# Issuing the gate weights of K tile 2 from SyncE's queue instead of ScalarE's

## The chip, the cores and the metric

One core of a Trainium2 chip. The metric is device time in microseconds (us) of one execution; most executions of this kernel lie within 0.5 us of 179.3, so a change of a tenth of a microsecond is near what can be seen at all.

Engines are called as the profile calls them: PE is TensorE's matmul, PEld its weight load, DVE is VectorE, ACT is ScalarE, POOL is GpSimd, SP is SyncE. "SPq" and "ACTq" lines are DMA issues by those sequencers: their time is the time of issuing, not that of the data.

## The reference, cut to what matters

```
x  = A_x                                # [1, 2048, 512] bf16
xn = layernorm(x)
out = x + S5(xn) + (silu(xn @ w_gate) * (xn @ w_up)) @ w_down
# S5: a complex diagonal recurrence over the 2048 rows: Bu = xn @ B, scan, @ C, + xn * Dskip
```

The kernel works in four chunks of 512 rows, each of four tiles of 128 rows (x0 to x3 in the first chunk). The dimension of 512 that is summed over in xn @ w_gate is cut into four "K tiles" of 128.

## The kernel before

The kernel is a graph of tasks. PE's and SP's tasks stay in the order of the program; those of DVE, ACT and POOL are put in order by a list scheduler with a cost model, before the program is built. The loads at the start, each a DMA with a semaphore of its own:

```python
x_load(0)
x_load(1)                                                     # SyncE, 128 KB each
act_q = [dma("ld_touch", ..., eng="act")]                     # 64 bytes
act_q.append(wg_load("a0", 0, 2, eng="act", ...))             # K tiles 0 and 1 of w_gate, 448 KB
x_load(2)
act_q.append(wg_load("a1", 2, 3, eng="act", ...))             # K tile 2, 224 KB: the line that changes
wg_load("a2", 3, 4)                                           # K tile 3, SyncE
x_load(3)
pload("ld_ldt", ...); pload("ld_lim", ...); pload("ld_lre", ...)   # three parameter rows, 1 KB each
dma("ld_wu0", ...); dma("ld_wg1", ...); dma("ld_wu1", ...)    # w_up, rest of w_gate, rest of w_up
dma("ld_x4", x_sb[:, 4:8, :], ...)                            # x of the second chunk, 512 KB
# [...] cut
dma("ld_bre", BT[:, 0], A_B_re, ..., xpose=True)              # transposing DMAs; each of them
dma("ld_bim", BT[:, 1], A_B_im, ..., xpose=True)              # waits for all DMAs before it
act_table(AF.Sqrt, (act_q[-1],))                              # ACT's first table, behind its last load
```

The opening of VectorE. Statistics of x2 (first half) stand ahead of x1's reciprocal and normalisation; the order is fixed:

```python
("r", 0, 0), ("n", 0, 0), ("b", 1, 0), ("b", 1, 1), ("s", 1, 0), ("b", 2, 0),   # b: statistics
("r", 1, 0), ("n", 1, 0), ("n", 1, 1), ("b", 2, 1), ...                         # r: reciprocal, n: normalise
```

The opening of PE: dummy matmuls, then x0's transposes, then for the 128 rows of x0 seven matmuls on each K tile, with x1's transpose placed after the 18th, and so on. The first chunk's matmuls on the rest of w_gate and on w_up follow, then those that read the transposed B (called `BT`).

The scheduler's model of a DMA halves the bandwidth for a queue that is not SyncE's:

```python
dma_free[e] = xs + t.nbytes / (_DMA_BW if e == "sp" else 0.5 * _DMA_BW)
```

Of the kernel before, what the change touches and what calls it, by code (L numbers as in the profile page):

```python
# [249 lines left out]
def bass_parallel_sum__ssm_conv_s5__swiglu_ffn__prompt_kernel(  # L250
# [32 lines left out]
    with es:  # L283
# [109 lines left out]
        def dma(name, dst, src, writes, nbytes, reads=(), after=(), out_=False, eng="sp", xpose=False, prio=0.0, order=(), **kw):  # L393
            after = tuple(after)
            if xpose:
                after = after + tuple(dma_tasks)
                fn = lambda e, dst=dst, src=src: e.dma_start_transpose(out=dst, in_=src)
                est, nb = 1900.0, int(nbytes * 1.2) + 140000
            else:
                if xp_state[0] is not None:  # L400
                    after = after + (xp_state[0],)
                fn = lambda e, dst=dst, src=src: e.dma_start(dst, src, **kw)
                est, nb = 330.0 + nbytes / 900.0, nbytes
            t = g.add(eng, fn, reads=reads, writes=writes, name=name, dma=True, after=after, out=out_, est=est, nbytes=nb, prio=prio, order=order)
            dma_tasks.append(t)
            if xpose:
                xp_state[0] = t
            return t
# [9 lines left out]
        def x_load(a, **kw):  # L418
            return dma("ld_x%d" % a, x_sb[:, a:a + 1, :], x_v[:, a:a + 1, :], [("x", a)], TILEB, **kw)

        def wg_load(nm, k0, k1, **kw):
            return dma("ld_wg" + nm, wg[:, k0:k1, 0:FG], wg_v[:, k0:k1, 0:FG], [("wg", nm)], (k1 - k0) * 128 * FG * 2, **kw)
# [4 lines left out]
        act_q = [dma("ld_touch", tch[0:16, 0:1], wg_v[0:128:8, 0:1, 0:2], [("tch",)], 16 * 4, eng="act")]  # L427
        act_q.append(wg_load("a0", 0, 2, eng="act", order=(act_q[-1],)))
        x_load(2)
        act_q.append(wg_load("a1", 2, 3, eng="act", order=(act_q[-1],)))  # L430
        wg_load("a2", 3, 4)
        x_load(3)
        pload("ld_ldt", 2, A_log_dt)
# [657 lines left out]
```

## Time and profile before

| | before |
|---|---|
| median of 3 runs | 179.53 us (179.03 to 179.59) |
| span of the profiled run | 177.5 us |
| PE busy | 173.9 us, 98% |
| DVE busy | 162.5 us, 92% |

From the page of the kernel before: the span, the busy times, and the chain of work that ended last, by engine.

```profile
span 177.5 us, 2421 instructions
PE 173.9 (98%) x927; PEld 83.9 (47%) x935; DVE 162.5 (92%) x284; ACT 87.8 (49%) x116; POOL 9.3 (5%) x22
...
## 4 chain that ended last, share of the span: by engine, by line
PE 98%; issue 0%; DVE 0%
```

The chain is PE almost alone: what doesn't give PE an earlier start or take a hole out of it changes nothing.

The timeline of before (start, duration, engine, line, operation, destination and source, count; in brackets the idle time ahead of it and what ended it):

```profile
1.22 0.97 ACTq L402 DMA_DIRECT2D wg<-in_B_w_gate_dram  x2
2.17 0.43 SPq L402 DMA_DIRECT2D wg<-in_B_w_gate_dram  x1
2.22 1.28 ACT L466 ACT_TABLE_LOAD   x1 [2.22 <-issue]
...
5.04 0.44 SPq L402 DMA_DIRECT2D wu<-in_B_w_up_dram  x1
5.45 0.21 DVE L522 BATCH_NORM_AGGREGATE mv<-st 128x2 f32<-128x12 f32 x1
5.71 1.17 PE L803 MATMUL pb<-xnT,wg 128*128 128x128 bf16 x18
5.92 0.43 DVE L512 BATCH_NORM_STATS2 st<-x_sb 128x6 f32<-128x256 bf16 x1 [0.26 <-DMA x_sb<-in_A_x_dram]
6.44 0.60 DVE L517 TENSOR_SCALAR xn_sb<-x_sb,mv,rstd 128x256 bf16<-128x256 bf16 x2
6.84 0.29 PE L582 MATMUL pb<-ident,xn_sb 128*128 128x128 bf16 x2
...
12.93 1.03 PE L759 MATMUL pb<-xnT,wg 128*128 128x512 bf16 x4
15.47 2.47 DVE L482 BATCH_NORM_STATS2 st<-x_sb 128x6 f32<-128x512 bf16 x4 [2.39 <-DMA x_sb<-in_A_x_dram]
15.52 2.12 SPq L397 DMA_TRANSPOSE BT<-in_A_B_re_dram  x1
19.66 2.14 SPq L397 DMA_TRANSPOSE BT<-in_A_B_im_dram  x1
23.83 1.79 SPq L397 DMA_TRANSPOSE xnT<-xn_sb  x1
```

What to see: at 5.92 DVE had stood 0.26 us for x2. Behind that statistic wait x1's reciprocal and normalisation (6.44), and for these PE waits before x1's transpose at 6.84. Its 18 gate matmuls started 56 ns apart from 5.71 on, the last at 6.65, so 0.14 us of PE is lost there (start to start in the trace, less the usual spacing). Lower down is a second chain, which is off PE: when x4-7 has landed, at 15.44, B_re's transposing DMA goes out, and when that has landed B_im's at 19.66. That one lands at 23.81, and PE wants it at 25.02.

### The profile page before, as it was taken

Reading aid. Unit: us, or ns where it says so; the run is one execution under the profiler, and the core shown is the slowest. Engines: PE = TensorE matmul, PEld = TensorE weight load, DVE = VectorE, ACT = ScalarE, POOL = GpSimd, SP = SyncE. Lnnn points to the kernel's source line nnn. Section 1 sums busy time; section 2 is a strip of 40 time slices with the busy share of each in tenths; the row PEclk is TensorE's granted clock in tenths of the full one; section 3 lists DMA queues with packets and bytes.
Section 4 is the critical chain, followed back from the end, with each engine's and each line's share of the span. In section 5 each row is a group of like instructions: output and inputs, shape, how many; then the busy total and the mean of one; then the engine's idle time right before and its main releaser. Section 6 shows DMA issues by size and latency. Waiting matters only on the chain.

```text
span 177.5 us, 2421 instructions
## 1 busy us (share of the span) xinstructions
PE 173.9 (98%) x927; PEld 83.9 (47%) x935; DVE 162.5 (92%) x284; ACT 87.8 (49%) x116; POOL 9.3 (5%) x22
## 2 busy tenths in 40 slices
PE   8999999999999999999999999999999999999994
PEld 2894444444444444444444444444444444444743
DVE  2865999899999999999999999999899999999933
ACT  4679979789999665034565560000965520000000
POOL 3022300040000000310000000000000000000000
PEclk9999999999999999999999999999999999999999
DMA  5992694664951000002700000002000000001022
GB/s 155 326 365 67 139 124 96 167 132 101 358 123 24 0 0 0 0 30 69 126 18 0 0 0 4 0 30 76 12 0 4 0 0 0 0 0 53 10 89 89
DMA packets 22966, 12.37 MB, mean 70 GB/s; under 512 B 15180, under 2 KB 22956, under 8 KB 22956
## 3 DMA queue, kind: packets, MB, share of 16 engines
q1 hardware_dynamic: 22508, 11.54, 25.0%
q10 hardware_dynamic: 448, 0.69, 1.2%
q8 instruction: 7, 0.11, 0.3%
q14 instruction: 3, 0.02, 0.0%
HBM read 6.46 MB, written 2.10 MB: 48 GB/s over the span
## 4 chain that ended last, share of the span: by engine, by line
PE 98%; issue 0%; DVE 0%
PE pb L759 36%; PE pb L959 21%; PE pb L876 16%; PE pb L972 15%; PE pb L803 4%; PE pb L477 3%; PE pb L839 2%; PE pb L849 1%; PE pb L582 1%; DVE x_sb L977 0%
## 5 line engine op out<-in xcount | busy, mean ns | idle before, releaser
L916 DVE TENSOR_TENSOR_SCAN rot<-sm,car,rot 128x512 bf16<-128x512 f32 x32 | 39.0, 1266 | 0.1
L959 PE MATMUL pb<-wd,hT 128*128 128x512 bf16 (+3 forms) x194 | 38.1, 355 | 0.2
L759 PE MATMUL pb<-xnT,wu 128*128 128x512 bf16 x160 | 37.3, 380 | 0.0
L759 PE MATMUL pb<-xnT,wg 128*128 128x512 bf16 x132 | 31.3, 380 | 0.0
L972 PE MATMUL pb<-W,hss 128*128 128x512 bf16 (+2 forms) x140 | 28.1, 355 | 0.2
L876 PE MATMUL pb<-xnT,BT 128*128 128x512 bf16 x128 | 28.1, 379 | 0.0
L959 PEld LDWEIGHTS pb<-wd,hT 128*128 128x128 bf16 (+1 forms) x198 | 18.5, 98 | 19.9
L759 PEld LDWEIGHTS pb<-xnT,wu 128*128 128x128 bf16 x160 | 15.6, 98 | 18.9 <-issue 0.2
L771 ACT ACTIVATE sg<-pb 128x1024 bf16<-128x1024 f32 x20 | 20.1, 1024 | 8.6 <-PE pb L759 7.7
L829 ACT ACTIVATE uf<-pb 128x1024 bf16<-128x1024 f32 x20 | 20.5, 1026 | 7.2 <-PE pb L759 5.9
L972 PEld LDWEIGHTS pb<-W,hss 128*128 128x128 bf16 x144 | 13.5, 98 | 14.3
L759 PEld LDWEIGHTS pb<-xnT,wg 128*128 128x128 bf16 x132 | 12.7, 98 | 15.7 <-ACT xn_sb L506 0.4
L876 PEld LDWEIGHTS pb<-xnT,BT 128*128 128x128 bf16 x128 | 12.5, 98 | 15.1
L883 ACT ACTIVATE u_sb<-pb 128x1024 bf16<-128x1024 f32 x16 | 16.2, 1017 | 5.4 <-PE pb L876 5.4
L977 DVE TENSOR_TENSOR x_sb<-pb,x_sb 128x512 bf16<-128x512 f32 (+2 forms) x18 | 11.0, 623 | 3.5 <-PE pb L972 3.5
L831 DVE TENSOR_TENSOR hT<-sg,uf 128x1024 bf16<-128x1024 bf16 x20 | 13.3, 680 | 0.0
L506 ACT ACTIVATE xn_sb<-x_sb,nmr,rstd 128x512 bf16<-128x512 bf16 x8 | 6.0, 804 | 9.2 <-DVE nmr L503 9.2
L858 ACT ACTIVATE sg<-pb 96x1024 bf16<-96x1024 f32 x2 | 2.0, 1013 | 17.1 <-PE pb L839 17.1
L482 DVE BATCH_NORM_STATS2 st<-x_sb 128x6 f32<-128x512 bf16 x12 | 7.4, 681 | 3.1 <-DMA x_sb<-in_A_x_dram 3.1
L907 DVE TENSOR_TENSOR rot<-rot,cosT 128x2048 bf16<-128x2048 bf16 x8 | 9.7, 1215 | 0.1
L907 DVE TENSOR_TENSOR rot<-rot,sin 128x2048 bf16<-128x2048 bf16 x8 | 9.7, 1216 | 0.0
L907 DVE TENSOR_TENSOR rot<-u_sb,cosT 128x2048 bf16<-128x2048 bf16 x8 | 9.7, 1216 | 0.0
(81 smaller groups left out, 144.3 us busy)
## 6 DMA issues: line engine op xcount, KB each, us to landing
out_dram<-x_sb SPq DMA_DIRECT2D x15, 128.0 KB, 1.7
x_sb<-in_A_x_dram SPq DMA_DIRECT2D x3, 512.0 KB, 6.9
wd<-in_B_w_down_dram SPq DMA_DIRECT2D x1, 1280.0 KB, 6.3
wu<-in_B_w_up_dram SPq DMA_DIRECT2D x1, 768.0 KB, 5.5
wu<-in_B_w_up_dram SPq DMA_DIRECT2D x1, 608.0 KB, 7.6
x_sb<-in_A_x_dram SPq DMA_DIRECT2D x4, 128.0 KB, 3.5
wg<-in_B_w_gate_dram SPq DMA_DIRECT2D x1, 480.0 KB, 6.4
wg<-in_B_w_gate_dram ACTq DMA_DIRECT2D x1, 448.0 KB, 4.0
```

Of the source, the lines that this page charges most:

```text
L482: return g.add("dve", lambda e, a=a: e.bn_stats(out=st[:, a, :], in_=x_sb[:, a, :]), reads=[("x", a)], writes=[("st", a)], name="bnst%d" % ...
L759: inst = e.matmul(pbank[0:fs, bk, :].rearrange("p (j t) -> p j t", j=4), lhsT=w[:, kt, i * 128:i * 128 + fs], rhs=xnT[:, c % 2, :, kt, :], ...
L771: g.add("act", lambda e: e.activation(out=sg[rows, sl, 0:n, :].rearrange("p a t -> p (a t)"), in_=pair_f32(rows, bk, 512 * n), func=AF.Sil ...
L829: g.add("act", lambda e: e.activation(out=uf[rows, ul, 0:n, :].rearrange("p a t -> p (a t)"), in_=pair_f32(rows, bk, 512 * n), func=AF.Ide ...
L831: g.add("dve", lambda e: e.tensor_tensor(out=hT[rows, hb, i0:i0 + n, :], in0=sg[rows, sl, 0:n, :], in1=uf[rows, ul, 0:n, :], op=ALU.mult), ...
L876: inst = e.matmul(pbank[:, bk, :].rearrange("p (j t) -> p j t", j=4), lhsT=BT[:, ri, kt, pt * 128:(pt + 1) * 128], rhs=xnT[:, c % 2, :, kt ...
L883: g.add("act", lambda e: e.activation(out=u_sb[:, us].rearrange("p r t -> p (r t)"), in_=pair_f32(slice(0, 128), b0), func=AF.Identity), r ...
L907: tt = lambda out, a, b, op, r, w, nm: g.add("dve", lambda e: e.tensor_tensor(out=out, in0=a, in1=b, op=op), reads=r, writes=w, name="%s_% ...
L916: g.add("dve", lambda e, A0=A0, A1=A1, k=k, ri=ri, pt=pt: e.tensor_tensor_scan(out=A1[:, k, ri, :], data0=rr[:, pt:pt + 1].to_broadcast([1 ...
L959: inst = e.matmul(pbank[:, bk, 0:nc_], lhsT=hT[0:fs, hb, i, lt * 128:(lt + 1) * 128], rhs=wd[0:fs, i, c0:c0 + nc_], start=(i == 0), stop=F ...
L972: inst = e.matmul(pbank[:, bk, 0:nc_], lhsT=hss[:, hb, pt, ri, lt * 128:(lt + 1) * 128], rhs=W12[:, ri, pt, c0:c0 + nc_], start=False, sto ...
L977: g.add("dve", lambda e, bk=bk, a=a, c0=c0, nc_=nc_: e.tensor_tensor(out=x_sb[:, a, c0:c0 + nc_], in0=pbank[:, bk, 0:nc_], in1=x_sb[:, a, ...
```

## The change

Its intent: take K tile 2 off ScalarE's queue, where it follows 448 KB, and put it in SyncE's behind x2.

```diff
         x_load(2)
-        act_q.append(wg_load("a1", 2, 3, eng="act", order=(act_q[-1],)))
+        wg_load("a1", 2, 3)
         wg_load("a2", 3, 4)
```

## The prediction

> **What bounds the kernel now.** TensorE. The page gives PE 98% of the 177.5 us span, granted clock 1.00; the chain that ended last is PE 98%. After its opening PE issues almost without a hole, and DVE (92% busy) is ahead of it: the last half of hss is done at 165.3 us, wanted at 168.1; the last W at 70.1, wanted at 74.5. So only what moves PE's opening (before 13 us) or makes a new hole counts.
>
> **The opening, from timeline and DMA landings.** An issue costs a sequencer 0.41 to 0.50 us. K tile 2 (224 KB) is issued by ScalarE at 1.7 us and lands 4.5 us later, at 6.2; its first matmul starts at 6.5, the weight load about 0.1 earlier. K tile 3 lands at 6.8, wanted at 7.1. x2 lands at 5.9, x3 at 7.2. VectorE, done with x1's statistics, stands 0.26 us waiting for x2 (the waits name it), so x1's normalisation, queued behind x2's statistics, comes late, and PE has a hole of 0.14 us before x1's transpose at 6.87.
>
> **What the change does.**
> - SyncE's queue gains an issue, 0.45 us. Everything behind slips: first w_up half 10.55 to 11.0 (wanted 13.8), rest of w_gate 11.9 to 12.4 (wanted 12.9), x4-7 15.5 to 15.9, and the transposing DMAs that follow: B_im lands at 23.8, wanted about 25; x chunk 1's transpose at 29.2, wanted at 31.1. Each keeps 0.5 us or more: nothing charged to PE.
> - ScalarE loses 0.49 us of issue, so the Sqrt table load starts at 1.7, not 2.2. Its first use waits for x0's statistics, done at 3.85; table and warm-up are done at 3.81 already. Worth nothing.
> - K tile 2 is issued at 2.2, not 1.7. From 3.0 to 6.5 us the DMA engines are saturated (share 1.0, about 370 GB/s), so the backlog, not the issue, sets the landing. The Trainium skill, "DMA: Bandwidth & Descriptors", section "Issuing engines are not separate DMA queues", says that DMAs of all issuers run on the same 16 engines and interleave. The trace agrees: between 4.5 and 5.25 us packets of both queues move, x2's and ScalarE's. With K tile 2 behind x2, x2 shares less: estimate from the packets' rates, x2 lands 0.2 to 0.5 us earlier (5.4 to 5.7); K tile 2, now ahead of K tile 3 instead of beside it, at 5.9 to 6.3; K tile 3 and x3 unchanged.
>
> **On the critical path.** If x2 is earlier, the 0.14 us hole goes: about -0.14 us. If K tile 2 lands after 6.4, PE stalls by the difference, at worst about 0.3.
>
> **Side effect.** The kernel orders its instructions by a cost model that halves the bandwidth of ScalarE's queue. There K tile 2 gets earlier and everything behind it on SyncE 0.7 us later, so DVE's and ACT's orders after 12 us may change. With 2 us or more of DVE slack I expect little; a bad order could cost some tenths.
>
> **Prediction.** 179.4 us, 178.9 to 180.2 eight times in ten. Faster by over 2%: 0.01; within 2%: 0.97; slower: 0.02.
>
> **What would show it.** DVE's wait for x2 gone or shorter; PE's hole before 6.87 gone; K tile 2 landing before 6.4; w_up landing about 0.45 us later; the DVE wait for x4-7 0.4 us longer; PE contiguous afterwards.
>
> **What would make it wrong.** SyncE's queue alone filling K tile 2 slower than two queues together (a PE hole at 6.4); w_gate's rest after 12.9; a new order that delays evacuations of PSUM, with PE waiting for ACT or DVE.

## The result

| | before | after |
|---|---|---|
| median of 6 runs | 179.48 us (179.03 to 179.59) | 179.17 us (179.01 to 179.59) |
| ratio to before (95% interval) | | 0.9993 (0.9977 to 1.001) |

A ratio here is the mean time of one kernel's runs over that of the other's of the same rounds, so it isn't quite the ratio of the medians. Executions over 1.5% slower than the fastest of the same kernel are left out of the means. The change is inside the noise. When both were run again later (below, `after_again` and `before_again`), after came out at 1.0008 and before, against itself, at 1.0007.

The profile after, page and timeline:

```profile
span 177.7 us, 2429 instructions
PE 174.5 (98%) x935; PEld 84.3 (47%) x935; DVE 162.7 (92%) x284; ACT 87.6 (49%) x116; POOL 10.2 (6%) x22
```

```profile
1.23 0.45 ACTq L402 DMA_DIRECT2D wg<-in_B_w_gate_dram  x1
1.71 1.28 ACT L466 ACT_TABLE_LOAD   x1 [1.71 <-PEq L1076]
2.18 0.91 SPq L402 DMA_DIRECT2D wg<-in_B_w_gate_dram  x2
...
5.46 0.21 DVE L522 BATCH_NORM_AGGREGATE mv<-st 128x2 f32<-128x12 f32 x1
5.51 0.44 SPq L402 DMA_DIRECT2D wu<-in_B_w_up_dram  x1
5.58 0.37 DVE L512 BATCH_NORM_STATS2 st<-x_sb 128x6 f32<-128x256 bf16 x1
5.80 1.38 PE L803 MATMUL pb<-xnT,wg 128*128 128x128 bf16 x18
6.23 0.60 DVE L517 TENSOR_SCALAR xn_sb<-x_sb,mv,rstd 128x256 bf16<-128x256 bf16 x2
7.01 0.28 PE L582 MATMUL pb<-ident,xn_sb 128*128 128x128 bf16 x2
...
13.09 1.03 PE L759 MATMUL pb<-xnT,wg 128*128 128x512 bf16 x4
16.18 2.47 DVE L482 BATCH_NORM_STATS2 st<-x_sb 128x6 f32<-128x512 bf16 x4 [2.01 <-DMA x_sb<-in_A_x_dram]
16.24 2.15 SPq L397 DMA_TRANSPOSE BT<-in_A_B_re_dram  x1
20.54 1.84 SPq L397 DMA_TRANSPOSE BT<-in_A_B_im_dram  x1
24.52 2.82 SPq L397 DMA_TRANSPOSE xnT<-xn_sb  x1
```

Three things stand in these lines.

1. The predicted step came true on VectorE: it no longer waits for x2 (5.58, no bracket), and x1 is normalised 0.2 us earlier. PE has no hole before x1's transpose either, but that alone shows little: PE arrives there at 7.01, when even the old queue's x1 (PE was released at 6.84 in before) would have been ready.
2. Yet PE reaches that transpose 0.17 us *later* (7.01 against 6.84), because its 18 matmuls start 0.09 us later, behind slower dummies, and take 1.38 us and not 1.17. In the trace the first five of them start 107 ns apart and the others 56 ns: the clock of TensorE rose only at 6.2 us. In before it had risen at 5.3, ahead of the first of them. The Trainium skill, "TensorE: Matmul & The Clock Gate", section "Part 1: The HAM clock gate (the "warmup" mystery)", says that the clock doubles after some 3.4 us of activity, at the end of a window that runs free of the kernel, so that the moment differs from run to run. The traces agree: 107 and 56 ns at 128 columns, and a rise at 5.3, 4.3, 6.2 and 6.5 us in four profiles of the two kernels, with the same dummy matmuls in front. The mean granted clock shows nothing of it (1.00 for both kernels), because time without a clock record counts as 1.00: the trace of before has its first record at 5.30 us, that of before_again at 4.33, each at the rise, and those of after and after_again have none, so the profile page of after lacks the row. There only the spacing tells.
3. From the first 512-column matmul (12.93 and 13.09) to the end of the span (177.5 and 177.7) both kernels take 164.6 us, although the scheduler put DVE's work in another order (by line, operation and tile 21 of its 284 instructions stand elsewhere in the trace). The order cost nothing.

And the slip: w_up was issued at 5.51 instead of 5.04, x4-7 landed 0.7 us later, and B_im with it. That is more than the issue's 0.47. Half of x4-7's 512 packets had started by 12.93 and 13.02 us in two looks at before, and by 13.53 and 13.27 in two at after, so the bulk slipped about as the issue did; but it lands with its last few packets, which started at 14.77 and 14.72, and at 15.67 and 15.26. Why this tail was longer in after isn't shown.

### The profile page after: what moved, and what is told of

It reads as the page before. It is cut to its first block, busy times and chain, and to the rows that moved or that the text cites. A ratio compares the mean times of both kernels' runs of the same rounds, so it can differ in the third digit from the quotient of the medians.

```text
span 177.7 us, 2429 instructions
## 1 busy us (share of the span) xinstructions
PE 174.5 (98%) x935; PEld 84.3 (47%) x935; DVE 162.7 (92%) x284; ACT 87.6 (49%) x116; POOL 10.2 (6%) x22
## 4 chain that ended last, share of the span: by engine, by line
PE 98%; DVE 0%; issue 0%
PE pb L759 36%; PE pb L959 21%; PE pb L972 16%; PE pb L876 16%; PE pb L803 4%; PE pb L477 3%; PE pb L839 2%; PE pb L849 1%; PE pb L582 1%; DVE x_sb L977 0%
## 5 line engine op out<-in xcount | busy, mean ns | idle before, releaser
L959 PE MATMUL pb<-wd,hT 128*128 128x512 bf16 (+3 forms) x198 | 38.8, 355 | 0.0
L907 DVE TENSOR_TENSOR rot<-u_sb,cosT 128x2048 bf16<-128x2048 bf16 x8 | 9.7, 1216 | 0.0
L907 DVE TENSOR_TENSOR rot<-u_sb,sin 128x2048 bf16<-128x2048 bf16 x8 | 9.7, 1216 | 0.0
```

The lines of the kernel that those rows point to most:

```text
L907: tt = lambda out, a, b, op, r, w, nm: g.add("dve", lambda e: e.tensor_tensor(out=out, in0=a, in1=b, op=op), reads=r, writes=w, name="%s_% ...
L959: inst = e.matmul(pbank[:, bk, 0:nc_], lhsT=hT[0:fs, hb, i, lt * 128:(lt + 1) * 128], rhs=wd[0:fs, i, c0:c0 + nc_], start=(i == 0), stop=F ...
```

## The experiments

Two questions were open. Is the step from x2 worth anything to the time, and if so, what takes it back? The moment of the clock's rise disturbs both, so most runs are of a delayed pair in which it falls before any real matmul.

### d_before, d_after, d_move, d_order: the clock's rise taken out; queue and orders apart

```diff
         streams = _schedule(g.tasks, engs)
+        dly = g.add("dve", lambda e: e.memset(rot[:, 0], 0.0), name="delay")   # nobody uses it; first load at 4.15 us, not 0.79
+        streams["dve"].insert(0, dly)
+        # [...] the first load of each queue waits for dly; writers of rot too
+        streams["pe"].insert(1, ...)        # nine more dummy matmuls, so that PE stays busy
```

In d_move the orders are those of before, and afterwards K tile 2's issue alone is moved to SyncE behind x2. In d_order the orders are those of after, and its issue is put back on ScalarE behind the first two K tiles.

> The kernel before, with every load held back by a 3.2 us fill on VectorE and TensorE kept busy with 9 more dummy matmuls, orders unchanged. Theory A (the spread of the runs, 179.0 to 179.6, is the moment at which TensorE's clock rises, 5.3 us in the profile of before, about 6.2 in that of after): the rise now falls before the first real matmul (about 9 us) in every run, so the runs lie within 0.25 us of each other, about 3.3 us above before (182.3 to 183.0), and the hole of about 0.14 us in TensorE ahead of x1's transpose is there in the profile. Rival: the spread comes from the DMA or from elsewhere and stays 0.5 us.

> The changed kernel with the same delay. Theory A with the step x2 of the prediction: no wait of VectorE for x2, no hole ahead of x1's transpose, and 0.10 to 0.20 us faster than d_before. Rival 1 (x2's earlier landing buys nothing, the 0.3 us between the medians was luck of the clock): within 0.05 us of d_before. Rival 2 (issues behind K tile 2 slip by 0.45 us and cost TensorE something): slower than d_before, with a new hole after 13 us of the undelayed time.

> Delayed; the instruction orders of before on all engines, only K tile 2's issue moved from ScalarE's queue to SyncE's behind x2. If the DMA move is the cause: as d_after within 0.06 us (0.10 to 0.20 faster than d_before). If the new orders of VectorE and ScalarE are the cause: as d_before.

> Delayed; the instruction orders of after on all engines, K tile 2's issue put back on ScalarE's queue behind the first two K tiles. If the DMA move is the cause: as d_before within 0.06 us, with the hole ahead of x1's transpose. If the new orders are the cause: as d_after.

| run | orders | K tile 2 issued by | five runs, us | mean |
|---|---|---|---|---|
| d_before | before | ScalarE | 182.35 182.39 182.80 182.67 182.69 | 182.58 |
| d_order | after | ScalarE | 182.44 182.38 182.33 182.48 182.37 | 182.40 |
| d_after | after | SyncE | 182.34 183.22 182.58 182.81 182.73 | 182.74 |
| d_move | before | SyncE | 182.75 183.29 182.42 182.68 182.71 | 182.77 |

In all four traces the clock had risen by 5.9 us and the first gate matmul began at 9.0, as meant. But two expectations fell. The runs didn't draw together (0.45 us for d_before, 0.88 for d_after), so the clock isn't the whole of the spread. And SyncE's queue wasn't 0.10 to 0.20 us faster: its ten runs have a mean of 182.75, those of ScalarE's queue 182.49, though the two ranges overlap. The orders have no effect of one sign: with K tile 2 on ScalarE the new ones are 0.18 us better, on SyncE they are equal.

The profile of d_move shows what a longer run holds. Its timeline (the line numbers are a few higher, from the added lines):

```profile
19.89 1.94 SPq L397 DMA_TRANSPOSE BT<-in_A_B_re_dram  x1
24.25 1.93 SPq L397 DMA_TRANSPOSE BT<-in_A_B_im_dram  x1
27.25 1.03 PE L878 MATMUL pb<-xnT,BT 128*128 128x512 bf16 x4
28.48 1.41 PEld L878 LDWEIGHTS pb<-xnT,BT 128*128 128x128 bf16 x8 [0.69 <-DMA BT<-in_A_B_im_dram]
28.48 1.69 PE L878 MATMUL pb<-xnT,BT 128*128 128x512 bf16 x7 [0.20 <-DMA BT<-in_A_B_im_dram]
```

PE does the four matmuls on B_re and then stands for B_im: 0.36 us, start to start. That is nearly all of the 0.40 us by which this run (182.75) is longer than d_before's profiled one (182.35): from the first 512-column matmul to the end it takes 164.99 us, and the profiles of the other three 164.59 to 164.60. This is a hole far behind the opening, at the end of the chain x4-7, B_re, B_im on SyncE's queue, the queue to which the change adds an issue. The prediction had looked at this chain and charged nothing for it. Two smaller facts from the opening of these four: the hole before x1's transpose was 0.00 in d_before and 0.07 us in d_order, so it isn't there in every run of the old queue; and with SyncE's queue K tile 3 landed at 10.27 and 10.29 instead of 9.95 and 9.91, and opened a hole of about 0.05 us in PE. The next pair doesn't repeat that (10.26 with SyncE's queue, without a hole, and 10.29 with ScalarE's), so it isn't shown to come from the change.

One flaw of this family: B_re's issue came 0.39 us after x4-7 had landed, in all four, and only 0.08 us after it in before and after (SyncE's fifteen waits stood in another order). So the delayed kernels are closer to this hole than the real ones: without the extra 0.31 us d_move's hole would have been about 0.05 (an estimate from these two numbers).

### p_before and p_after: the wait for B taken out as well

```diff
+        # ten dummy matmuls (2.2 us) ahead of the first matmul that reads B
+        streams["pe"].insert(streams["pe"].index(b0), pad)
-                for d in t.deps:
+                for d in sorted(t.deps, key=lambda d: d.idx):     # waits in the order of the loads
```

> d_before with two more things, the same in both of this pair: ten dummy matmuls (about 2.2 us) ahead of the first matmul that reads B, so that no wait for the transposed B can show, and SyncE's waits put in the order of the loads. If the late B (hole of 0.36 us in d_move's profile) is what spread d_before's runs (182.35 to 182.80), they now lie within 0.2 us, about 184.5. If the spread comes from the opening, it stays 0.4 us.

> The changed kernel with the same delay, dummies and wait order. What is left between the two is the opening alone. The prediction's step (x2's earlier landing closes a hole of 0.14 us) would give 0.10 to 0.20 us faster. My theory now (the hole ahead of x1's transpose is there in some runs only, 0.14, 0.03 and 0.07 us in three profiles of the old queue, and K tile 3, now 0.3 us later, opens another of 0.05): equal within 0.08 us, and a spread under 0.2 us, while d_after spread over 0.88.

Measured: p_before 184.71, 184.77, 184.80, 184.88 (mean 184.79); p_after 184.72, 184.75, 184.78, 184.81, 184.91 (mean 184.79); both 1.0311 times before. The two are equal to 0.01 us, and the spread is 0.17 and 0.19 us. With the wait for B out of reach the difference between the queues is gone, and so is most of the spread. Two things were done at once here, the dummies and the order of the waits (on every engine); both keep PE from waiting for B, but they weren't tried apart. In p_after's profile B_im's transposing DMA took 5.7 us (23.80 to 29.52) instead of about 4.1; PE wanted it at 30.50, which without the dummies would have been 2.2 us earlier. So by estimate from these numbers that run would have stood for 1.2 us.

Timelines of the opening, first p_before, then p_after:

```profile
9.28 0.43 DVE L512 BATCH_NORM_STATS2 st<-x_sb 128x6 f32<-128x256 bf16 x1 [0.19 <-DMA x_sb<-in_A_x_dram]
10.21 0.29 PE L583 MATMUL pb<-ident,xn_sb 128*128 128x128 bf16 x2
```

```profile
9.12 0.43 DVE L512 BATCH_NORM_STATS2 st<-x_sb 128x6 f32<-128x256 bf16 x1
10.08 0.28 PE L583 MATMUL pb<-ident,xn_sb 128*128 128x128 bf16 x2
```

The wait for x2 and the hole behind it (0.07 us) are there in p_before and not in p_after; the profiled run of p_before was the slowest of its four. The step is real, but it is worth less than the spread of a run.

### p_x2late: is it x2's landing that makes the hole?

```diff
+        # on SyncE's queue x2's issue goes behind K tile 2's
+        streams["sp"].remove(x2)
+        streams["sp"].insert([t.name for t in streams["sp"]].index("ld_wga1") + 1, x2)
```

> p_after with x2's issue put behind K tile 2's on SyncE's queue. x2 lands about 0.6 us later than in p_after (9.7 instead of 9.09). The prediction's mechanism: VectorE waits for x2, and the hole ahead of x1's transpose is 0.3 to 0.6 us, no other; 0.3 to 0.6 us slower than p_after (185.1 to 185.4; ratio to before 1.033 to 1.035 against 1.0311). Rival (x2's landing is not what makes that hole): hole and time as p_after's.

Measured: 184.96, 185.12, 185.36, 185.51 us, ratio to before 1.0330, so 0.44 us slower than p_after (by the means; p_after is of other rounds). Timeline:

```profile
9.35 0.43 DVE L512 BATCH_NORM_STATS2 st<-x_sb 128x6 f32<-128x256 bf16 x1 [0.36 <-DMA x_sb<-in_A_x_dram]
10.28 0.28 PE L583 MATMUL pb<-ident,xn_sb 128*128 128x128 bf16 x2
```

The profiled run, the fastest of the four, has a wait of 0.36 us for x2 and a hole of 0.25 us in PE at x1's transpose, a little under what was expected; x2 landed at 9.33 and not 9.7. The mechanism of the prediction is shown: x2's landing sets this hole. The change moved x2 by a few tenths in the good direction, where the hole ends at zero; this run moved it in the other, where the hole grows.

### slip: more of what the change costs

```diff
+        # three more loads of 64 bytes on SyncE's queue, ahead of w_up
+        streams["sp"].insert(at, sl)
```

> The changed kernel with three more tiny loads (64 bytes each) issued on SyncE ahead of w_up: everything behind slips by another 1.2 to 1.4 us (the change itself slips it by 0.45). If a slip of SyncE's queue costs TensorE through the transposed B: x4-7 lands about 17.4 us, B_im about 25.8, some 0.6 us after TensorE wants it (25.2), a hole among the first eight matmuls that read B, and the runs 0.4 to 1.0 us above before (ratio 1.002 to 1.006). If the slip is free, as the prediction had it: ratio 0.998 to 1.002 and no hole.

Measured: 180.08 to 180.72, median 180.39 us, ratio 1.0058 (1.0042 to 1.0075). From its waits (engine, line and tile that waited, what for: us in total, times, longest):

```profile
PEld pb L759 <- DMA wg<-in_B_w_gate_dram: 0.7, 1, 0.7
PEld pb L876 <- DMA BT<-in_A_B_im_dram: 0.6, 1, 0.6
PE pb L759 <- DMA wg<-in_B_w_gate_dram: 0.5, 1, 0.5
```

The time is as expected, but the place only half so. The first and larger hole, 0.66 us, is at the rest of w_gate, which landed at 13.38 where PE wanted it at about 12.8; behind that B_im still cost 0.27 us, although the first hole had already given it 0.66 us. Part of that may be the experiment's own: with its three added waits SyncE issued B_re 0.27 us behind x4-7's landing, where after has 0.08. So a further slip of SyncE's queue by 1.4 us (w_up issued at 6.91 instead of 5.51) costs about 1.0 us. The change's slip of 0.45 us is of the same kind, and in the profiles of after it stays inside the slack.

### after_again and before_again: the two unaltered kernels once more

> The changed kernel unaltered, for more runs beside before and another profile. Median 179.0 to 179.5, ratio to before 0.997 to 1.003; the moment of TensorE's clock rise differs from the 6.2 us of the first profile; B_im lands 0.3 to 1.0 us before its first matmul (0.67 in the first profile; 1.21 in before).

> The kernel before unaltered, against itself: how far apart the same kernel comes out, and a second profile. Ratio 0.998 to 1.002, runs over 0.4 us; the hole ahead of x1's transpose between 0 and 0.15 us, B_im's margin 0.7 to 1.4 us.

Measured: after_again 179.21 to 179.57, median 179.33, ratio 1.0008 (0.9993 to 1.0024); before_again 179.00 to 179.84, median 179.36, ratio 1.0007 (0.9990 to 1.0025). The same kernel against itself comes out as far from one as the change does. The expectations held but for B_im's margin in before_again, 2.03 us instead of at most 1.4. The four profiles of the unaltered kernels side by side (us; landings from the trace):

| | before | before_again | after | after_again |
|---|---|---|---|---|
| TensorE's clock rose at | 5.3 | 4.3 | 6.2 | 6.5 |
| K tiles 0 and 1 landed | 5.20 | 6.24 | 5.08 | 5.02 |
| x2 landed | 5.89 | 6.48 | 5.41 | 5.34 |
| hole of PE before x1's transpose | 0.14 | 0.13 | 0 | 0 |
| K tile 2 landed | 6.17 | 6.89 | 6.22 | 5.94 |
| K tile 3 landed | 6.76 | 7.47 | 6.81 | 6.55 |
| x4-7 landed | 15.44 | 15.11 | 16.16 | 16.35 |
| B_im landed | 23.81 | 23.57 | 24.51 | 24.61 |
| B_im wanted by PE | 25.02 | 25.60 | 25.18 | 25.32 |
| B_im's margin | 1.21 | 2.03 | 0.67 | 0.70 |
| time of the profiled run | 179.25 | 179.84 | 179.43 | 179.57 |

before_again's profile caught the slowest of its six runs, and a third cause: K tiles 0 and 1 landed a microsecond late, and PE waited for them, 0.63 us more than the usual spacing. One line of its waits:

```profile
PEld pb L803 <- DMA wg<-in_B_w_gate_dram: 0.7, 1, 0.7
```

From the first 512-column matmul on, the four profiles agree: it starts at 12.93, 13.52, 13.09 and 13.23 us, and 164.58 to 164.61 us follow. So all that sets these four executions apart lies in the opening, and none of them lost time to B.

### relief and split_relief: trying to keep the gain without the slip

SyncE is given back one issue: the load of one parameter row (1 KB) goes to ScalarE, which idles after 6.3 us. split_relief also loads K tiles 0 and 1 as two DMAs, in the issue slot that the change freed on ScalarE.

```diff
+        for nm, behind in (("ld_lim", "xTev0_1"),):
+            p = next(t for t in streams["sp"] if t.name == nm)
+            streams["sp"].remove(p)
+            streams["act"].insert([t.name for t in streams["act"]].index(behind) + 1, p)
+            p.eng = "act"
```

> The changed kernel with one parameter load (Lambda_im) issued by ScalarE in its idle time after 6.3 us instead of by SyncE: SyncE's queue has as many issues as before, K tile 2 stays behind x2. x4-7 lands near 15.5 us, B_im's margin back at 1.0 to 1.5 us. If the slip is what the change pays with, the runs are tighter than the changed kernel's and 0.05 to 0.2 us below; ratio to before 0.997 to 1.000. If not: as the changed kernel, ratio 1.000 to 1.001.

> relief, and the first two K tiles as two loads on ScalarE (the issue slot that the change freed), so that K tile 0 lands first, 0.4 to 0.6 us earlier than the pair did. It is meant to beat both: in runs as the second profile of before, where the pair landed at 6.24 us and TensorE stood 0.63 us, the first matmul would not wait. Expected ratio 0.996 to 0.999, runs between 178.8 and 179.3. If the opening is not what makes the slow runs: as relief.

Measured: relief 180.45 to 181.61 us in five runs, ratio 1.0093 (a sixth, 183.87, was slow); split_relief 180.68 to 181.04, ratio 1.0087. Both are *slower* by about 1.6 us: the expectation failed altogether. Timeline of relief:

```profile
5.97 0.51 SPq L402 DMA_DIRECT2D wu<-in_B_w_up_dram  x1
5.99 1.12 ACTq L402 DMA_DIRECT2D prow<-in_A_Lambda_im_dram  x1
...
11.30 0.21 DVE L556 STREAM_TRANSPOSE prT<-prow 128x32 bf16<-128x32 bf16 x1 [1.96 <-DMA prow<-in_A_Lambda_im_dram]
12.01 0.28 PE L582 MATMUL pb<-ident,xn_sb 128*128 128x128 bf16 x2 [1.23 <-DVE xn_sb L517]
```

The 1 KB was issued at 5.99 and landed at 11.22. VectorE stood 1.96 us for it with x3's normalisation behind it, and PE lost 1.39 us before x3's transpose (1.84 us in split_relief). I had taken ScalarE's queue, which was empty, to be a way past SyncE's backlog. Here it wasn't. In the trace the first of its sixteen 64-byte packets moved at 9.92 us: after the first 960-byte packets of w_gate's rest (SyncE, issued at 5.43, from 8.82 on) and just before the first 1216-byte ones of w_up's second part (SyncE, issued at 5.97, from 10.11 on). split_relief has the same order (8.62, 9.70, 10.12). So in both runs the loads began in the order of issue across the two queues. This bears on the change itself: x2 and K tile 2 were issued within 0.01 us of each other before, and K tile 2 0.47 us after x2 afterwards. Its later issue may be what brought x2 forward, rather than the other queue; no run issued it late from ScalarE. B_im's margin in relief (2.14 us) says nothing of the slip, since PE came late. And x4-7 landed at 16.12, not near 15.5, though it was issued as early as in before: the tail of its packets again (half of them had started by 13.02, the last at 15.62). In split_relief K tile 0 landed at 4.58 and the first matmul didn't wait, but whether that would pay without this mistake wasn't tried. No version beats before and after.

## Why the prediction was right, point by point

- **The bound and the total.** PE bound the kernel before and after, and the time stayed within 0.2% of before, as predicted (179.4, 178.9 to 180.2; measured 179.17). That the first medians differ by 0.31 us is luck: the second ones are 179.36 and 179.33.
- **Where x2 and the K tiles land.** Predicted x2 at 5.4 to 5.7, K tile 2 at 5.9 to 6.3, K tile 3 unchanged; measured 5.41, 6.22 and 6.81 (6.76 before), and in the second profile of after 5.34, 5.94 and 6.55. The skill's statement on which it rested ("DMA: Bandwidth & Descriptors", "Issuing engines are not separate DMA queues") agrees with these traces: between 4.5 and 5.25 us of before, packets of x2 from SyncE and of w_gate from ScalarE moved side by side.
- **The hole of 0.14 us.** The mechanism is shown by p_x2late, where it grows; its absence in the two profiles of after agrees, but PE came late there. The *size* was overcounted as a gain of the whole run: the hole was 0.14, 0.13, 0.07, 0.07 and 0.00 us in the five profiles with K tile 2 on ScalarE (before, before_again, d_order, p_before, d_before; the expectation of p_after put 0.03 for the last, the trace has none), and when the clock rises late, as in both profiles of after, PE isn't at that place early enough to need x2. In the pair freed of both disturbances the gain was 0.00 us (184.79 and 184.79).
- **ScalarE's freed issue is worth nothing.** Right: the table load moved from 2.22 to 1.71, and PE's first transpose from 4.83 to 4.84.
- **Nothing charged for SyncE's slip.** Right for what the profiles of after show, no hole behind 13 us, but argued too lightly: I read each slack from one profile and took it as fixed, and took the issue's 0.45 us for the slip of the landings, where x4-7 came 0.72 us later, and 0.91 in the second profile. B_im's margin was 1.21 and 2.03 us in two looks at before and 0.67 and 0.70 in two at after; where it was used up (d_move, slip) PE stood 0.36 and 0.27 us. Whether some runs of the unaltered after lose time there isn't shown: no profile caught one. The delayed family suggests it (0.26 us in the means, gone in the p pair).
- **The new orders.** Changed as foreseen, without effect: 164.6 us from the first 512-column matmul to the end in both.
- **Signs that didn't come.** DVE's wait for x4-7 was to be 0.4 us longer than 2.39 and was 2.01, under the new order; w_up's first half was to land 0.45 us later than 10.52 and landed at 10.79, and at 10.12 in the second profile.
- **Not foreseen.** The moment of the clock's rise, which differed by 2 us between looks at the same kind of kernel. In the first profile of after it cost more than the change could have brought: five matmuls at 107 instead of 56 ns, about 0.25 us by that count (an estimate).

What stays open: how the spread of 0.5 us of the unaltered kernels divides among the clock, K tiles 0 and 1, and B_im. The first two were caught in profiles of the unaltered kernels, but a profile shows one run; B_im was caught only in d_move and slip.

## What to carry to other kernels

Here the load that was moved to another queue got no new bandwidth; it traded places. Count what moves up (here x2, by half a microsecond) and also every chain behind the place where it went in. Read a slack from more than one profile before calling it free, and when the gain you expect is a tenth of a microsecond, first build a pair in which the known disturbances (the clock's rise, a load at the edge) can't fall, and compare there.

## What the Trainium skill lacked or had wrong

- "DMA: Bandwidth & Descriptors", section "Queues, rings and completion order", says that each DMA engine goes round the queues it has work for, packet by packet, and that SyncE's and ScalarE's queues have no descriptor generator of their own. From this going round one would expect a small load on an idle queue to be quick. In relief 1 KB on ScalarE's otherwise empty queue took 5.2 us from issue to landing behind SyncE's backlog, its first packet 3.9 us after the issue. The page doesn't say that loads of the two queues can start in the order of their issue, as these did.
- No page gives the time from a transposing DMA's issue to its landing; "DMA: Bandwidth & Descriptors", section "Latency and other measured facts", has an effective bandwidth. Here B_re and B_im, 512 KB each, took 3.9 to 4.4 us, and B_im once 5.7 us.
- "TensorE: Matmul & The Clock Gate", section "Part 1: The HAM clock gate (the "warmup" mystery)", puts the rise at around 4 us into sustained activity, give or take 0.5 us. Its steps of 107 and 56 ns are right here; its spread is too small: in the four profiles of the unaltered kernels the rise came 3.5 to 5.7 us after the first dummy matmul (0.83 us). The page warns that clock records can be unreliable; it doesn't say that they can be missing, as in 6 of these 14 traces, the two of after among them.
